# The low halves of eight input-weight blocks made by VectorE instead of TensorE, in a kernel with a written-out order

## The chip, the cores and the metric

The kernel runs on one core of one Trainium2 chip. The metric is the device time of one execution in microseconds (us), as the median of several runs. Engines are named as in the profile: PE is TensorE (PEld its weight loads), DVE is VectorE, ACT is ScalarE, POOL is GpSimd, SP is SyncE. "L603" is line 603 of the kernel. A difference of about 0.5% (3.3 us) is what a measurement of this kernel can tell from no change.

## The reference

A delta-rule linear attention runs over 768 steps for 4 batches and 8 heads of width 48. Its output, 3072 tokens of 384 values, goes through a feed-forward layer with 2048 hidden values:

```python
for t in range(S):                                   # 768 steps
    y[:, :, t] = einsum('bhd,bhde->bhe', q_t, state)
    v_old = einsum('bhde,bhd->bhe', state, k_t)      # k normalised
    state = state + b_t * outer(k_t, v_t - v_old)
x = y as (3072, 384)
h = x @ w_in                                         # 384 x 2048
g = h * erf(softplus(h))
return g @ w_out                                     # 2048 x 384
```

## The kernel before

**Two halves of the work.** The 768 steps are cut into 12 chunks of 64. For each chunk and each batch there is one step of a chain (48 steps): `chain_u`, `chain_s` and `chain_y` multiply by the state on PE (L461, L474, L488), and DVE or ACT take the results out (L467, L482, L480, L493). Ahead of each chunk a triangular system is solved row by row on POOL (`solve_row`, L363 and L364), and `merge_e` (PE, L400) puts the solved blocks together. Four chain steps give 256 tokens, a group; there are 12 groups. For a group `x_hi` (ACT, L661) and `x_lo` (DVE, L666) split the tokens into a high and a low half of 16 bits each, the tiles `xh` and `xl` (`xh0` is group 0). `ffn1` (PE, L678) computes h in 16 blocks of 128 hidden values, nine matmuls each; `e_sp` and `e_erf` (ACT, L704 and L709) apply softplus and erf, each after a load of its function table (L128) where the other stands in the engine; `e_mul`, `e_split` and `e_rest` (DVE L713; DVE L724 or ACT L722; POOL or DVE L728) form g and its two halves; `ffn2` (PE, L739 to L741) multiplies them by the output weights and sums over the 16 blocks.

**Weights.** An fp32 product is made of products of 16-bit halves, so both weight matrices are split into a high and a low half too. They come in as pairs of 32-bit words, twelve pieces each (`w_load`, DMA on SP), and are put together by `w_mask` (ACT, L539), `w_low` and `w_bits` (DVE, L543 and L547). `w_sum` (ACT, L554) and `w_max` (DVE, L558) find the largest magnitude, `w_scale` the power of two to scale by. Then each of the 16 blocks (128 x 384) is split:

- `w_hi` makes the high half `h`: mode 5 on DVE (L588), the other modes used here on ACT (L590).
- `w_lo` makes the low half, a scaled minus h. In modes 3 and 5 PE does it first: `w_dif` multiplies the block by a scaled identity `dg` in fp32 (L603) and adds the block's high half times a negative identity `ng` (L604), into a PSUM bank `wd_in` of the pool that also holds the two `ph` banks of `ffn1`; ACT then copies it to the low half (L611). In mode 0, DVE does it in one two-operand pass from SBUF (L615).

The halves of block i are written over the staged fp32 values of block i-1, so `w_hi` of a block waits until the block before has been read by `w_dif` or `w_lo`. The list `LMI` gives the mode of each of the 16 blocks of `w_in`, `LMO` of `w_out` (all 0):

```python
m = (LMI if nm == "in" else LMO)[i]
...
on(ti, w_hi, nm, i, m)
if m > 2:
    on(ti + 0.04, w_dif, nm, i)
on(ti + 0.08, w_lo, nm, i, m)
```

**Order.** Every piece of work is an event `on(time, function, arguments)`. The events are sorted by time, and then put into the order that the table `ORDER` gives; the instructions go to the engines in that order, and each engine runs its own in order. Tiles of pools wait for their readers. During the first 80 us PE is filled up with matmuls that compute nothing (`warm` and `fill`, L143), each at its place in the order.

Of the kernel before, what the change touches and what calls it, by code (L numbers as in the profile page):

```python
# [37 lines left out]
WARM = 8  # L38
WU = 150
WO = 0.6  # L40
WD = 0.4
RI = "HLHLHLHLHLLL"
RO = "HLHLHLHLHLLL"
LMI = [5, 3] * 8
LMO = [0] * 16
WG = 3
LID = 0.12
LOD = 0.25
HQ = (0, 4)
SPA = (2, 6)  # L50
# [22 lines left out]
def delta_ffn_kernel(ctx, tc, kT, qT, ktok, vtok, btok, w_in, w_out, cst, out):  # L73
# [825 lines left out]
    for nm, t in (("in", us(42)), ("out", WO + WD * (NRW - 1) + 1.2)):  # L899
# [4 lines left out]
        for i in range(NFF):  # L904
            m = (LMI if nm == "in" else LMO)[i]
            ti = t + 0.2 + (LID if nm == "in" else LOD) * i
# [42 lines left out]
    ev.sort(key=lambda e: (e[0], e[1]))  # L949
    if ORDER:  # L950
        ev = [ev[i] for i in ORDER]
    E = mybir.EngineType
# [45 lines left out]
```

## Time and profile before

| | |
|---|---|
| runs | 657.1, 657.86, 655.23 us; median 657.1 us |
| profiled execution | 655.3 us; span of the profile 653.5 us |
| PE, DVE, ACT, POOL busy | 96%, 73%, 72%, 56% of the span |
| granted PE clock, mean | 0.995 |
| first `ffn1` matmul of group 0 | 96.74 us from the start |
| first `ffn2` matmul | 128.76 us |

The span is the time between the first and last recorded instruction; the execution's own time is 1.8 us longer. Busy shares are means over stages: up to about 66 us weights are put together and the first chunks solved, from there to 97 us `w_in` is split and the first tokens are made, from 97 to 129 us the first `ffn1` blocks run while `w_out` is scaled and the third chunk solved, and after that chain and feed-forward layer run side by side to the end.

### The profile page before, as it was taken

The page shows a single profiled execution, that of the slowest core. Times are in us where ns is not written, and L with a number is a line of the kernel's source. Part 1 is how long each engine was busy: PE and PEld are TensorE (multiplying, and loading weights), DVE is VectorE, ACT ScalarE, POOL GpSimd, SP SyncE. Part 2 cuts the span into 40 slices and gives each one's busy share as a digit, 9 for nine tenths or more (in the row PEclk, how much of TensorE's full clock was granted, in tenths as well). Part 3 has the DMA queues.
Part 4 walks back from the last instruction along what each step waited for, and adds up shares of the span by engine and source line. Part 5 has one row for each costly group of instructions (what it writes and reads, how often), then busy time and mean ns, then how long its engine had stood idle before and what let it go on. Part 6 is the DMA issues. An engine that isn't in the chain of part 4 may idle for free.

```text
span 653.5 us, 22870 instructions
## 1 busy us (share of the span) xinstructions
PE 624.5 (96%) x9866; PEld 481.5 (74%) x9866; DVE 479.3 (73%) x1032; ACT 470.3 (72%) x696; POOL 364.3 (56%) x524
## 2 busy tenths in 40 slices
PE   5969999999999999999999999999999999999996
PEld 4646667788678788678787777787787787777764
DVE  4999887898889877688975868775676767565451
ACT  1468789999678765775677677688782879778851
POOL 4190388779997359694279952158986131302421
PEclk9999999999999999999999999999999999999999
DMA  9857853471113742304625034441004410000101
GB/s 233 315 188 231 194 140 87 102 151 42 41 50 98 158 73 64 75 3 106 143 52 132 2 83 94 104 84 45 16 2 87 111 33 2 1 14 2 25 17 44
DMA packets 76421, 56.19 MB, mean 86 GB/s; under 512 B 57185, under 2 KB 66529, under 8 KB 76321
## 3 DMA queue, kind: packets, MB, share of 16 engines
q1 hardware_dynamic: 76320, 54.74, 34.2%
q8 instruction: 77, 1.26, 0.8%
q14 instruction: 24, 0.19, 0.1%
HBM read 42.14 MB, written 12.58 MB: 84 GB/s over the span
## 4 chain that ended last, share of the span: by engine, by line
PE 56%; DVE 20%; ACT 13%; DMA 3%; issue 3%; POOL 2%; SPq 2%; POOLq 0%; ACTq 0%; DVEq 0%
PE ph L678 17%; PE pr L739 7%; PE pr L741 7%; PE pr L740 7%; ACT L128 4%; DVE H L713 3%; PE pc L488 2%; PE pq L251 2%; ACT L L704 2%; PE pc L461 2%; PE pg L251 2%; ACT L L709 2%; PE pc L474 2%; PE pm L426 1%; DVE z L467 1%
## 5 line engine op out<-in xcount | busy, mean ns | idle before, releaser
L678 PE MATMUL ph<-xh,w_in 128*128 128x256 f16 x1152 | 207.1, 273 | 2.6 <-ACT L L704 2.0
L678 PEld LDWEIGHTS <-w_in 128*128 128x128 f16 x1728 | 164.9, 98 | 30.0 <-issue 3.6
L728 POOL TENSOR_TENSOR L<-H,L 128x512 f16<-128x512 f32 x72 | 86.8, 1213 | 150.6 <-DVE L L724 69.0
L128 ACT ACT_TABLE_LOAD x131 | 168.1, 1283 | 2.3
L678 PE MATMUL ph<-xl,w_in 128*128 128x256 f16 x576 | 157.0, 273 | 0.0
L740 PE MATMUL pr<-w_out,L 128*128 128x384 f16 x384 | 125.2, 326 | 0.6 <-DVE w_out L615 0.6
L739 PE MATMUL pr<-w_out,L 128*128 128x384 f16 x384 | 125.4, 327 | 0.0
L741 PE MATMUL pr<-w_out,L 128*128 128x384 f16 x384 | 125.2, 326 | 0.0
L448 POOL TENSOR_TENSOR z<-v,nm 64x192 f32<-64x192 f32 x96 | 58.6, 610 | 102.1 <-DMA v<-vtok 64.9
L704 ACT ACTIVATE L<-ph,xct 128x512 f32<-128x512 f32 x96 | 65.8, 687 | 49.2 <-DVE H L691 46.1
L364 POOL TENSOR_TENSOR xb<-xb,tmp 128x31 f32<-128x31 f32 (+15 forms) x155 | 93.4, 603 | 12.1
L363 POOL TENSOR_TENSOR tmp<-gb,xb 128x31 f32<-128x31 f32 (+15 forms) x155 | 89.7, 578 | 12.1 <-DMA gb<-d 2.3
L713 DVE TENSOR_TENSOR H<-H,L 128x512 f32<-128x512 f32 x96 | 78.5, 824 | 20.9 <-ACT L L709 20.2
L691 DVE TENSOR_SCALAR H<-ph 128x512 f32<-128x512 f32 x72 | 49.1, 684 | 38.9 <-PE ph L678 35.2
L709 ACT ACTIVATE L<-L 128x512 f32<-128x512 f32 x96 | 58.3, 626 | 0.8
L741 PEld LDWEIGHTS <-L 128*128 128x128 f16 x384 | 37.6, 98 | 25.6 <-issue 0.8
L739 PEld LDWEIGHTS <-L 128*128 128x128 f16 x384 | 37.5, 98 | 21.4
L740 PEld LDWEIGHTS <-L 128*128 128x128 f16 x384 | 37.6, 98 | 20.2
L467 DVE TENSOR_TENSOR z<-pc,ga 64x192 f32<-64x192 f32 x80 | 28.4, 355 | 21.4 <-PE pc L461 19.8
L482 DVE TENSOR_TENSOR z<-pc,z 48x192 f32<-48x192 f32 x72 | 25.4, 353 | 16.7 <-PE pc L474 10.8
L724 DVE CAST L<-H 128x512 f16<-128x512 f32 x72 | 36.4, 510 | 1.6
L661 ACT ACTIVATE xh<-pt,xsx 64x128 f16<-64x128 f32 (+1 forms) x72 | 25.9, 394 | 14.3 <-DVE xsx L528 7.4
(159 smaller groups left out, 983.1 us busy)
## 6 DMA issues: line engine op xcount, KB each, us to landing
raw_in<-w_in SPq DMA_DIRECT2D x12, 512.0 KB, 7.6
raw_out<-w_out SPq DMA_DIRECT2D x12, 512.0 KB, 5.5
d<-A SPq DMA_DIRECT2D x20, 256.0 KB, 3.2
kpg<-kT SPq DMA_DIRECT2D x24, 192.0 KB, 3.9
k<-ktok SPq DMA_DIRECT2D x12, 384.0 KB, 4.1
qp<-qT SPq DMA_DIRECT2D x24, 192.0 KB, 4.0
v<-vtok SPq DMA_DIRECT2D x48, 96.0 KB, 3.3
out<-ob SPq DMA_DIRECT2D x48, 96.0 KB, 2.2
```

The source lines that it names most:

```text
L128: se.add_instruction(mybir.InstLoadActFuncSet(name=nc.get_next_instruction_name(), act_func_set_id=i, ins=[], outs=[]))
L363: ge.tensor_tensor(tv, G[:, s, s + 1:].unsqueeze(1).broadcast_to([P, ncol, nr]), Xv[:, :, s:s + 1].broadcast_to([P, ncol, nr]), op=ALU.mult)
L364: ge.tensor_tensor(Xv[:, :, s + 1:], Xv[:, :, s + 1:], tv, op=ALU.add)
L448: ge.tensor_tensor(zz[j % 6][h1, :, hb, :], vt[j][h1], st[c]["nm"][h1, cs].unsqueeze(2).broadcast_to([C, NP, D]), op=ALU.mult)
L678: te.matmul(ph, w[:, i, kt * P:kt * P + P], G[x][:, :, ksl], start=(m == 0), stop=(m == 8))
L704: se.activation(unit("L", g, u), G["ph", u], AF.Softplus, bias=0.0, scale=G["ct"])
L709: se.activation(Lu, Lu, AF.Erf, bias=0.0, scale=1.0)
L713: ve.tensor_tensor(Hu, Hu, unit("L", g, u), op=ALU.mult)
L728: (ge if (g * NFF // EU + u) % GLM else ve).tensor_tensor(G["gl", u], unit("H", g, u), G["gh", u], op=ALU.subtract)
L739: te.matmul(G["po"][a], gh[:, o, asl], wout_h[:, i, :], start=(i == 0), stop=False)
L740: te.matmul(G["po"][a], gh[:, o, asl], wout_l[:, i, :], start=False, stop=False)
L741: te.matmul(G["po"][a], gl[:, o, asl], wout_h[:, i, :], start=False, stop=(i == NFF - 1))
```

## The change

Blocks 0 to 7 of `w_in` are split as before. For blocks 8 to 15 the mode becomes 0: the high half is made by ACT (L590, where half of these blocks had it on DVE, L588), the low half by DVE's pass L615; `w_dif` and the copy L611 of these blocks are gone. All events stand in a new order.

```diff
-ORDER = (42,7,36,3,5,63,4,14,13,15,77,72,6,9,65,49,37,58,48,57,...
+ORDER = (1,442,7,42,5,3,4,27,360,14,77,6,56,273,72,15,9,65,37,49,...
...
-LMI = [5, 3] * 8
+LMI = [5, 3] * 4 + [0] * 8
```

`ORDER` had 2531 entries and has 2523: eight `w_dif` events less. By instructions: PE L603 and L604 from 16 to 8 blocks each; DVE L588 from 8 to 4 and L615 from 16 (all of `w_out`) to 24; ACT L590 for `w_in` from 8 to 12, L611 from 16 to 8, and table loads from 131 to 123, since `e_sp` and `e_erf` of neighbouring blocks stand together in more places. POOL and SP issue the same instructions as before, in another order.

On PE, just ahead of the first `ffn1` matmul: `wd_in9` to `wd_in11` are the differences of blocks 9 to 11 (two pieces, the rows between them are chain matmuls). Before:

```order
L603 MATMUL wd_in9_1616<-w_in_100,dg_103 128x384
L604 LDWEIGHTS ng_104
L604 MATMUL wd_in9_1616<-w_in_100,ng_104 128x384
L474 MATMUL pr2_83<-z5_99,k1_124 48x48 x8
L603 MATMUL wd_in10_1645<-w_in_100,dg_103 128x384
```

```order
L603 MATMUL wd_in11_1676<-w_in_100,dg_103 128x384
L604 LDWEIGHTS ng_104
L604 MATMUL wd_in11_1676<-w_in_100,ng_104 128x384
L678 LDWEIGHTS w_in_100
L678 MATMUL ph0_1_1686<-xh0_1619,w_in_100 128x256
```

After, at the same place (`pt` is the transposed tokens of group 0, from L644 and L645):

```order
L474 MATMUL pr1_82<-z4_98,k1_125 48x48 x8
L644 MATMUL pt0_1_1620<-ident_84,y2_1517 128x128
L645 MATMUL pt0_1_1620<-ident_84,y2_1517 64x128
L644 MATMUL pt0_1_1620<-ident_84,y3_1550 128x128
L645 MATMUL pt0_1_1620<-ident_84,y3_1550 64x128
L488 MATMUL pr2_83<-z5_99,qp1_0_88 64x48
```

```order
L474 MATMUL pr2_83<-z5_99,k1_125 48x48 x8
L678 LDWEIGHTS w_in_100
L678 MATMUL ph0_1_1682<-xh0_1615,w_in_100 128x256
L678 LDWEIGHTS w_in_100
L678 MATMUL ph0_1_1682<-xl0_1616,w_in_100 128x256
```

Before, twelve `w_dif` stand ahead of the first L678 and four behind it; after, all eight stand ahead of it, and between the last of them and L678 there is chain and token work alone.

On DVE, around the low half of group 0's tokens (`xl0`; `xsx0` is their scale). Before:

```order
L467 TENSOR_TENSOR z5_99<-pr2_83,ga0_254 64x4x48 x2
L588 TENSOR_SCALAR w_in_100<-w_in_100,sc_in_110 128x384
L666 SCALAR_TENSOR_TENSOR xl0_1620<-pt0_0_1499,xsx0_1561,xh0_1619 128x2x128
L666 SCALAR_TENSOR_TENSOR xl0_1620<-pt0_0_1499,xsx0_1561,xh0_1619 64x2x64 x2
L482 TENSOR_TENSOR z2_96<-pr1_82,z4_98 48x4x48 x2
L666 SCALAR_TENSOR_TENSOR xl0_1620<-pt0_1_1576,xsx0_1561,xh0_1619 128x2x128
L666 SCALAR_TENSOR_TENSOR xl0_1620<-pt0_1_1576,xsx0_1561,xh0_1619 64x2x64 x2
```

After:

```order
L467 TENSOR_TENSOR z5_99<-pr2_83,ga0_268 64x4x48 x2
L615 SCALAR_TENSOR_TENSOR w_in_100<-w_in_100,sc_in_110 128x384
L666 SCALAR_TENSOR_TENSOR xl0_1616<-pt0_0_1596,xsx0_1564,xh0_1615 128x2x128
L666 SCALAR_TENSOR_TENSOR xl0_1616<-pt0_0_1596,xsx0_1564,xh0_1615 64x2x64 x2
L615 SCALAR_TENSOR_TENSOR w_in_100<-w_in_100,sc_in_110 128x384
L666 SCALAR_TENSOR_TENSOR xl0_1616<-pt0_1_1620,xsx0_1564,xh0_1615 128x2x128
L666 SCALAR_TENSOR_TENSOR xl0_1616<-pt0_1_1620,xsx0_1564,xh0_1615 64x2x64 x2
L615 SCALAR_TENSOR_TENSOR w_in_100<-w_in_100,sc_in_110 128x384
```

Two of the new passes L615 stand between the pieces of `xl0` where one L588 and a chain pair L482 stood; L482 has moved behind.

On ACT, up to the first erf of a block that `ffn2` needs first (`L0_0` is blocks 0 and 1 of group 0). Before:

```order
L590 ACTIVATE w_in_100<-w_in_100,sc_in_110 128x384
L611 CAST w_in_100<-wd_in14_1975 128x384
L273 COPY qp1_0_88<-pq3_0_1989 64x512
L273 COPY qp1_1_89<-pq3_0_1989 64x512
L590 ACTIVATE w_out_101<-w_out_101,sc_out_114 128x384
L128 ACT_TABLE_LOAD
L709 ACTIVATE L0_0_1742<-L0_0_1742 128x512
```

After:

```order
L590 ACTIVATE w_out_101<-w_out_101,sc_out_114 128x384
L128 ACT_TABLE_LOAD
L704 ACTIVATE L0_2_2085<-ph0_4_1987,xct0_1565 128x512
L128 ACT_TABLE_LOAD
L709 ACTIVATE L0_2_2085<-L0_2_2085 128x512
L722 CAST L0_1_1818<-H0_1_1806 128x512
L709 ACTIVATE L0_0_1745<-L0_0_1745 128x512
```

Two table loads, a softplus, an erf of another block (`L0_2`) and a cast now stand directly ahead of this erf. From the last instruction of `xh0` to this erf there were 36 instructions on ACT and are 42.

2 lines of the change are left out of this document (1 added, 1 removed).

## The prediction

> **What bounds the kernel now.** I read the page's first lines first, then the table of windows cut at three milestones: 65.70 us, when DVE has the largest magnitude of `w_in`; 96.75, the first `ffn1` matmul; 128.76, the first `ffn2` matmul. Columns of the windows: stretch, its length, busy time and instructions of PE, PEld, DVE, ACT, POOL, granted clock, DMA share, GB/s.
>
> ```profile
> PE 624.5 (96%) x9866; PEld 481.5 (74%) x9866; DVE 479.3 (73%) x1032; ACT 470.3 (72%) x696; POOL 364.3 (56%) x524
> PE 56%; DVE 20%; ACT 13%; DMA 3%; issue 3%; POOL 2%; SPq 2%; POOLq 0%; ACTq 0%; DVEq 0%
> 65.70:96.75 31.05, 29.68 (x492) 20.28 (x492) 25.84 (x61) 25.06 (x57) 19.03 (x33) 1.00 0.68 166
> 96.75:128.76 32.01, 30.13 (x441) 24.98 (x440) 26.22 (x67) 31.41 (x50) 25.84 (x44) 1.00 0.42 98
> 128.76:653.50 524.74, 512.97 (x7574) 399.44 (x7571) 372.90 (x781) 380.12 (x538) 293.73 (x413) 1.00 0.28 61
> ```
>
> PE is busy 96% of the span, and idle 1.4, 1.9 and 11.8 us in the three stretches, so work taken from it should shorten the run. But in the second stretch ACT is busier than PE: 31.41 of 32.01 us. Whether PE's saving shows depends on that. The matmuls around the first milestone, by PE's timeline (start, length, what):
>
> ```profile
> 77.68 1.14 PE L143 MATMUL warm<-zero 128*128 128x384 f16 x6
> 93.75 0.91 PE L603 MATMUL wd_in<-w_in,dg 128*128 128x384 f32 x2
> 94.50 0.33 PE L604 MATMUL wd_in<-w_in,ng 128*128 128x384 f16 x1
> 94.76 0.67 PE L461 MATMUL pr<-z,xm 128*64 128x48 f32 x16
> 96.74 0.27 PE L678 MATMUL ph<-xh,w_in 128*128 128x256 f16 x1
> 78.70:96.75 18.05, 17.59 (x279) 11.87 (x278) 15.12 (x37) 15.00 (x36) 14.51 (x27) 1.00 0.60 144
> ```
>
> The last filler ends near 78.7, and from there PE is busy 17.59 of 18.05 us: it sets the first `ffn1` before. One `w_dif` costs it 94.76 - 93.75 = 1.01 us. At the second milestone the engines hand over just in time (erf on ACT, product, cast and rest on DVE, `ffn2` on PE):
>
> ```profile
> 93.78 1.10 ACT L661 ACTIVATE xh<-pt,xsx 128x256 f16<-128x256 f32 x3
> 94.90:121.75 26.85, 24.97 (x390) 20.10 (x389) 22.41 (x57) 26.35 (x40) 23.79 (x40) 1.00 0.41 94
> 119.83 1.28 ACT L128 ACT_TABLE_LOAD   x1
> 121.12 0.63 ACT L709 ACTIVATE L<-L 128x512 f32<-128x512 f32 x1
> 126.25 0.68 DVE L713 TENSOR_TENSOR H<-H,L 128x512 f32<-128x512 f32 x1
> 126.96 0.61 DVE L724 CAST L<-H 128x512 f16<-128x512 f32 x1
> 127.61 0.88 DVE L728 TENSOR_TENSOR L<-H,L 128x512 f16<-128x512 f32 x1
> 128.76 0.33 PE L739 MATMUL pr<-w_out,L 128*128 128x384 f16 x1
> ```
>
> `xh0` is done at 94.88; the first erf that `ffn2` needs ends 121.75, after 26.87 us in which ACT is busy 26.35; DVE then takes until 128.49.
>
> **The change, priced.** The prices are the means of groups (line, operation, count; busy, mean ns; idle before and its releaser):
>
> ```profile
> L603 PE MATMUL wd_in<-w_in,dg 128*128 128x384 f32 x32 | 14.2, 525 | 1.9 <-ACT L L704 1.9
> L604 PE MATMUL wd_in<-w_in,ng 128*128 128x384 f16 x16 | 5.2, 326 | 0.9 <-DVE w_in L588 0.9
> L611 ACT CAST w_in<-wd_in 128x384 f16<-128x384 f32 x16 | 7.6, 475 | 4.0 <-PE wd_in L604 3.9
> L588 DVE TENSOR_SCALAR w_in<-w_in,sc_in 128x384 f16<-128x384 f32 x8 | 4.4, 550 | 0.1
> L590 ACT ACTIVATE w_in<-w_in,sc_in 128x384 f16<-128x384 f32 x8 | 4.9, 611 | 1.3 <-PE wd_in L603 1.3
> L615 DVE SCALAR_TENSOR_TENSOR w_out<-w_out,sc_out 128x384 f16<-128x384 f32 x16 | 14.1, 884 | 4.8 <-ACT w_out L590 4.8
> L128 ACT ACT_TABLE_LOAD x131 | 168.1, 1283 | 2.3
> L482 DVE TENSOR_TENSOR z<-pr,z 48x192 f32<-48x192 f32 x8 | 2.8, 352 | 0.1
> L543 DVE TENSOR_SCALAR raw_out<-raw_out 128x512 int32<-128x512 int32 x12 | 7.4, 620 | 0.0
> ```
>
> In all: PE loses 8 x 1.01 = 8.1 us; DVE gains 8 x 0.884 - 4 x 0.55 = 4.9; ACT loses 8 x 0.475 - 4 x 0.611 = 1.4, and eight table loads, 10.3. The counts below are from the two orders.
>
> *Up to the first `ffn1`.* DVE has three instructions fewer ahead of the largest magnitude (one L543, two L467, which cost about as much as L482): 0.62 + 0.71 = 1.3 us earlier. From there to the last `xl0` it has 62 instead of 60: three L615 (2.65), one L543 (0.62) and two L467 (0.71) more, two L588 (1.10) and two L482 (0.71) fewer, +2.2. ACT has 51 in both to the last `xh0`, by kinds +1.2. PE has 8 `w_dif` there instead of 12, 4.0 us less, and fillers stand as far as the sixth `w_dif`. So PE no longer sets this point, DVE does: 25.84 + 2.2 = 28.0 us of work instead of 31.05 of stretch. If it waited for nothing, the milestone would come 31.05 - 28.0 + 1.3 = 4.3 early; if all its waits stayed, 2.2 - 1.3 = 0.9 late. PE's pieces between still release it, so a good part of the waits stays: I take 1.0 us early, range -3 to +1.
>
> A wait is new here: `w_hi` of blocks 9 to 15 (ACT) waits for L615 of the block before (DVE), and the pieces of `xh0` are queued behind three of them. The two alternate, `xh` 1.10 and L590 0.61 on ACT beside `xl` 1.09 and L615 0.88 on DVE:
>
> ```profile
> 65.55 0.16 DVE L558 TENSOR_REDUCE m_in<-mx_in 128x1 f32<-128x4 f32 x1
> 95.65 1.09 DVE L666 SCALAR_TENSOR_TENSOR xl<-pt,xsx,xh 128x256 f16<-128x256 f32 x3
> ```
>
> Per half, ACT needs 1.71 us and DVE 1.97; so ACT's wait is covered by DVE's own work: 0, at most one L590, 0.6, inside the range above.
>
> *First `ffn1` to first `ffn2`.* ACT has 42 instructions from the last `xh0` to that erf instead of 36: two table loads, a softplus, an erf, a cast and four copies among those added, five L611 among those gone; by prices +4.3. ACT had 0.5 us idle here, so the erf ends 31.2 us after `xh0` instead of 26.87. Behind it DVE needs only its three instructions, 0.68 + 0.61 + 0.88 and their starts, 2.2 to 2.9, where it took 6.7 (121.75 to 128.49). 31.2 + 2.6 = 33.8, against 128.49 - 94.88 = 33.6: no change. So of the four `w_dif` that PE loses here nothing is won. DVE has 70 instructions ahead of this L728 instead of 65, +4.0 us (five L615 4.42, two L482 0.71, less two L588 1.10), and was idle 32.01 - 26.22 = 5.8: it fits, with 1.8 left. I take 0, range -1 to +2, the upper end if DVE's own waits don't shrink.
>
> *Behind the first `ffn2`.* PE's work is the same. What waits there is short (PE's waits, engine and line waited for: us, times, mean):
>
> ```profile
> PE ph L678 <- ACT L L704: 2.0, 3, 1.0
> PE pr L740 <- DVE w_out L615: 0.6, 1, 0.6
> ```
>
> Ten of ACT's table loads fewer lie here, 12.8 us, off the path but for the first of these waits; I take -0.7 (about a third of it), range -4 to +4 since the order is new for 1,500 events and 11.8 us of PE's idle time is the stock both ways.
>
> Sum: -1.0 + 0 - 0.7 = -1.7; the profiled execution took 655.3 us (span 653.5 and 1.8 around it), so 653.6 by it. It stands 1.8 below the median of its runs, 657.1, and the measured time should be 657.1 - 1.7 = 655.4.
>
> **Rivals.** *The saving comes through.* If ACT's and DVE's work beside PE gives way, as PE's 96% suggests, all 8.1 us show: 657.1 - 8.1 = 649.0. For it speaks that PE was saturated up to 96.75; against it, ACT's 31.41 of 32.01 us right behind. It needs ACT's chain to the erf to be shorter than I add up, by about 5 us, or the loss to be taken back from the 11.8 us later.
>
> *POOL and DVE hold each other up; slower.* The same pass L615 took 0.61 us at 123.66, when POOL stood idle, and 1.59 at 129.01, beside POOL's L282:
>
> ```profile
> 123.66 0.61 DVE L615 SCALAR_TENSOR_TENSOR w_out<-w_out,sc_out 128x384 f16<-128x384 f32 x1
> 129.01 1.59 DVE L615 SCALAR_TENSOR_TENSOR w_out<-w_out,sc_out 128x384 f16<-128x384 f32 x1
> 128.93 2.81 POOL L282 TENSOR_TENSOR qp<-qp,mask 64x512 f32<-64x512 f32 x2
> L364 POOL TENSOR_TENSOR xb<-xb,tmp 128x31 f32<-128x31 f32 (+15 forms) x31 | 18.2, 587 | 2.4
> L363 POOL TENSOR_TENSOR tmp<-gb,xb 128x31 f32<-128x31 f32 (+15 forms) x31 | 16.9, 544 | 2.4
> 122.65 0.27 POOL L364 TENSOR_TENSOR xb<-xb,tmp 128x31 f32<-128x31 f32 x1
> 135.03 0.24 PE L400 MATMUL pe<-T,A 32*32 32x32 f32 x2
> ```
>
> The eight new passes fall among the 62 rows of the solve (66 to 130 us). If each holds POOL up for its own 0.61, the solve ends 8 x 0.61 = 4.9 late, at 127.8 instead of 122.9, and the merge at 135.03, which follows it through two trips of DMA, and the chain behind it follow. With the 1.0 won ahead: 657.1 + 4.9 - 1.0 = 661.0. It decides once the solve's delay exceeds what stands between its end and the merge, 12.1 us, less those trips, which this trace does not split. Against it: the mean of L615 is 0.884, so most of the passes lose 0.3 and not 1.0, and DVE's L588, taken away four times, are passes too.
>
> [...]
>
> *Stalls of the new order*, anywhere, of either sign: a part of the ranges above; as a case of its own, 3 us or more either way, 0.07.
>
> **How the numbers follow.** My forecast 0.45 (its own range 652 to 658.5, some 3 us either way: 2 from the first `ffn1` and 2 from the idle time behind `ffn2`, added as independent), the saving whole 0.28, slower by POOL and DVE 0.20, other stalls 0.07. Predicted 655.4. Low end 648: it takes in 649.0; high end 662: it takes in 661.0; outside remain the larger stalls and the far tails of each, under 2 in 10. About 0.5%, 3.3 us, is what can be told from no change: faster is below 653.8, slower above 660.4. Faster: the saving case 0.26, a fifth of my forecast 0.09, half the stalls 0.03: 0.38. Slower: most of the POOL case 0.14, 0.03 of mine, 0.03 of stalls: 0.20. Same: 0.42.
>
> **What would show it.** In the profile after: first L678 near 95.7 and no PE saturation ahead of it; PE's idle time between first `ffn1` and first `ffn2` up from 1.9 to about 6 us, waiting for ACT or DVE; the first L739 near 127.8; PE busy near 616, and its share lower; idle time behind it still near 11 to 12 us. If L739 comes at 121 to 123, the saving case holds; if the last L364 ends past 127 and L400 past 139, the POOL case. L615 for `w_in` well above 0.9 us speaks for that too. I would be wrong if ACT reached the erf sooner than by its count, or if the new order changed PE's 11.8 us of later idle time by several us.

## The result, and the profile after

The changed kernel is slower: median 665.0 us (662.12 to 669.29, 4 runs) against 656.16 for the kernel before (its three runs above and a fourth, 654.69), ratio 1.0104, 95% interval 1.0063 to 1.0145. On another chip it took 667.86, ratio 1.0129 (1.0088 to 1.0170). The forecast was 655.4, faster by 1.7, with a range of 648 to 662.

The profiled execution took 662.1 us, span 660.3. The page's first line and its chain by engine:

```profile
PE 626.5 (95%) x9842; PEld 481.9 (73%) x9842; DVE 487.6 (74%) x1036; ACT 459.7 (70%) x684; POOL 367.8 (56%) x524
PE 45%; POOL 19%; DVE 14%; ACT 11%; DMA 5%; issue 5%; SPq 1%; POOLq 0%; DVEq 0%; ACTq 0%
```

PE has 8 us less to do, yet it is busy 626.5 us where it was busy 624.5: some of its work took longer, at a lower clock (mean granted clock 0.978, before 0.995). The same three stretches as before, cut at the largest magnitude of `w_in` (64.74), the first `ffn1` (94.92) and the first `ffn2` (130.45):

```profile
64.74:94.92 30.18, 29.37 (x511) 20.51 (x506) 24.60 (x60) 25.14 (x53) 19.82 (x33) 1.00 0.73 196
94.92:130.45 35.53, 27.91 (x432) 23.29 (x429) 29.45 (x75) 34.45 (x53) 28.30 (x44) 1.00 0.35 84
130.45:660.34 529.89, 516.14 (x7572) 400.39 (x7572) 382.38 (x782) 366.45 (x526) 294.09 (x412) 0.99 0.27 60
```

The second is 3.5 us longer than before, and PE's idle time in it went from 1.9 to 7.6 us; ACT is as full as it was (34.45 of 35.53). The third is 5.1 us longer, at a mean clock of 0.99. What PE waited for in the second stretch:

```profile
101.33 0.27 PE L678 MATMUL ph<-xh,w_in 128*128 128x256 f16 x1 [1.24 <-ACT L L704]
115.76 0.27 PE L678 MATMUL ph<-xh,w_in 128*128 128x256 f16 x1 [1.41 <-ACT L L704]
123.78 0.27 PE L678 MATMUL ph<-xh,w_in 128*128 128x256 f16 x1 [1.67 <-ACT L L704]
129.04 0.39 PE L678 MATMUL ph<-xh,w_in 128*128 128x256 f16 x2 [0.81 <-DVE w_in L615]
132.12 0.34 PE L741 MATMUL pr<-w_out,L 128*128 128x384 f16 x1 [1.17 <-DVE L L728]
```

Three times `ffn1` waits for a softplus on ACT, which frees a `ph` bank; at 129.04 it waits for the new pass L615 of the last block. At the hand-over ACT's erf ends at 126.71 (first row below). DVE's five passes behind it and POOL's four mask multiplications (`gram_p2`, L282) follow:

```profile
126.09 0.62 ACT L709 ACTIVATE L<-L 128x512 f32<-128x512 f32 x1
126.75 0.69 DVE L713 TENSOR_TENSOR H<-H,L 128x512 f32<-128x512 f32 x1 [3.74 <-ACT L L709]
127.36 1.63 DVE L615 SCALAR_TENSOR_TENSOR w_in<-w_in,sc_in 128x384 f16<-128x384 f32 x1
128.91 1.48 DVE L724 CAST L<-H 128x512 f16<-128x512 f32 x1
130.43 1.64 DVE L728 TENSOR_TENSOR L<-H,L 128x512 f16<-128x512 f32 x1
131.99 1.22 DVE L638 TENSOR_TENSOR xco<-xm,c_out 128x1 f32<-128x1 f32 x1
126.96 6.22 POOL L282 TENSOR_TENSOR qp<-qp,mask 64x512 f32<-64x512 f32 x4
```

The cast took 0.61 before and takes 1.48, the rest 0.88 and now 1.64: each of the last four ends 0.0 to 0.6 us behind the end of one of the four L282. Even a pass over one column (L638) takes 1.22, where the median of its twelve is 0.15. Before, L282 began at 128.93, behind this hand-over. Then PE's clock (the column ahead of the last two):

```profile
128.00:130.00 2.00, 1.17 (x10) 0.60 (x7) 2.00 (x2) 1.95 (x7) 1.93 (x2) 1.00 0.40 62
130.00:132.00 2.00, 0.50 (x2) 0.11 (x2) 1.97 (x3) 1.12 (x1) 1.85 (x3) 1.00 0.87 178
132.00:134.00 2.00, 1.20 (x6) 0.61 (x7) 2.00 (x4) 0.00 (x0) 1.93 (x2) 0.80 0.23 51
134.00:136.00 2.00, 2.00 (x15) 0.97 (x15) 1.95 (x6) 1.19 (x2) 0.59 (x2) 0.50 0.71 111
138.00:140.00 2.00, 2.00 (x27) 1.64 (x25) 1.74 (x3) 1.95 (x4) 0.00 (x0) 0.50 0.17 39
140.00:142.00 2.00, 2.00 (x39) 1.65 (x39) 1.97 (x4) 1.56 (x3) 1.25 (x2) 0.99 0.00 0
```

After six microseconds in which PE was busy 2.9, its clock is halved until 140, about 6.8 us (below, such a stretch is called a dip): a "busy" PE that does less, an L741 taking 0.52 us in it and 0.33 behind it.

The stretches of the main profiles side by side, in us, worked out from the starts of the same instructions in each trace, the last column to the end of the last one (the time up to the largest magnitude of `w_in` is left out: it lies between 64.7 and 71.4 in the profiles of both orders, from one execution to the next):

| | to first `ffn1` | to third `ffn2` matmul | to second group's first `ffn2` | to the last `ffn2` |
|---|---|---|---|---|
| before | 31.0 | 32.4 | 52.3 | 467.0 |
| changed | 30.2 | 37.2 | 54.2 | 469.0 |
| changed, again | 30.8 | 37.4 | 54.2 | 469.4 |
| edit alone (below) | 29.9 | 34.8 | 51.3 | 467.1 |
| new order in the front alone (below) | 32.2 | 36.6 | 51.7 | 468.8 |

The two profiles of the changed kernel agree within 0.6 us in every stretch, so +4.8 between the first `ffn1` and the third `ffn2` matmul and +1.9 behind it can be read. The long rest scatters more: ten profiles with the order of before there have 466.3 to 471.7 (mean 468.6), seven with the new order 469.0 to 472.1 (mean 470.7). So some 2 us more there show as a mean, not in one profile.

### The profile page after: what moved, and what is told of

Its sections match the earlier page's. It is cut to its first block, busy times and chain, and to the rows that moved or that the text cites. A ratio compares the mean times of both kernels' runs of the same rounds, so it can differ in the third digit from the quotient of the medians.

```text
span 660.3 us, 22811 instructions
## 1 busy us (share of the span) xinstructions
PE 626.5 (95%) x9842; PEld 481.9 (73%) x9842; DVE 487.6 (74%) x1036; ACT 459.7 (70%) x684; POOL 367.8 (56%) x524
## 4 chain that ended last, share of the span: by engine, by line
PE 45%; POOL 19%; DVE 14%; ACT 11%; DMA 5%; issue 5%; SPq 1%; POOLq 0%; DVEq 0%; ACTq 0%
PE ph L678 14%; POOL xb L364 7%; POOL tmp L363 7%; PE pr L739 6%; PE pr L740 5%; PE pr L741 5%; ACT L128 4%; POOL L L728 2%; PE warm L143 2%; PE pg L251 2%; POOL z L448 2%; DMA d<-A 2%; DVE H L713 2%; ACT L L709 2%; PE pc L488 2%
## 5 line engine op out<-in xcount | busy, mean ns | idle before, releaser
L678 PE MATMUL ph<-xh,w_in 128*128 128x256 f16 x1152 | 206.4, 273 | 7.7 <-ACT L L704 5.4
L678 PEld LDWEIGHTS <-w_in 128*128 128x128 f16 x1728 | 165.6, 98 | 36.0 <-issue 6.9
L728 POOL TENSOR_TENSOR L<-H,L 128x512 f16<-128x512 f32 x72 | 87.9, 1229 | 170.7 <-DVE L L724 79.6
L678 PE MATMUL ph<-xl,w_in 128*128 128x256 f16 x576 | 157.2, 273 | 0.3 <-DVE xl L666 0.3
L741 PE MATMUL pr<-w_out,L 128*128 128x384 f16 x384 | 125.6, 327 | 1.2 <-DVE L L728 1.2
L364 POOL TENSOR_TENSOR xb<-xb,tmp 128x31 f32<-128x31 f32 (+15 forms) x155 | 95.6, 617 | 12.2
L713 DVE TENSOR_TENSOR H<-H,L 128x512 f32<-128x512 f32 x96 | 76.3, 803 | 28.5 <-ACT L L709 21.8
L691 DVE TENSOR_SCALAR H<-ph 128x512 f32<-128x512 f32 x72 | 49.1, 685 | 28.9 <-PE ph L678 21.1
L741 PEld LDWEIGHTS <-L 128*128 128x128 f16 x384 | 37.6, 98 | 27.4 <-DVE L L728 1.6
L724 DVE CAST L<-H 128x512 f16<-128x512 f32 x72 | 45.3, 633 | 1.4
L143 PE MATMUL warm<-zero 128*128 128x384 f16 x158 | 34.1, 366 | 2.2 <-issue 2.2
```

Of the source, the lines that this page charges most:

```text
L364: ge.tensor_tensor(Xv[:, :, s + 1:], Xv[:, :, s + 1:], tv, op=ALU.add)
L678: te.matmul(ph, w[:, i, kt * P:kt * P + P], G[x][:, :, ksl], start=(m == 0), stop=(m == 8))
L713: ve.tensor_tensor(Hu, Hu, unit("L", g, u), op=ALU.mult)
L728: (ge if (g * NFF // EU + u) % GLM else ve).tensor_tensor(G["gl", u], unit("H", g, u), G["gh", u], op=ALU.subtract)
L741: te.matmul(G["po"][a], gl[:, o, asl], wout_h[:, i, :], start=False, stop=(i == NFF - 1))
```

## Experiments

Beside these runs the kernel before was run 23 to 35 times on each chip, with medians of 659.0 to 660.3 us, 3 to 4 us above that of the first four. Ratios are against the runs on the same chip, and times in us are to be read through them.

**The edit, or the order?** The first kernel has the old order with the new modes; of each of blocks 8 to 15 `w_lo` stands where its `w_dif` stood:

```diff
-LMI = [5, 3] * 8
+LMI = [5, 3] * 4 + [0] * 8
 order of events, for i = 8 ... 15:
-w_dif in i
+w_lo in i
...
-w_lo in i
```

> The order of before with the new modes: blocks 8 to 15 have their low half by DVE's pass L615, standing where their w_dif stood; no other event moves. Theory, the order and not the modes made the loss: the mask multiplications stand behind the hand-over as before, the first ffn2 matmul comes at 127 to 130 us, and the time is 652 to 658 us, within 0.5% of before. Rival, the passes on DVE cost by themselves (4.9 us more on DVE, ACT's high half waiting for DVE block by block): 660 to 666 us. Rival, PE's 8 us come through with the old order: 648 to 650 us.

Measured: 659.95 us against 659.72, ratio 1.0002 (0.9976 to 1.0028). As forecast by the ratio; the hand-over is clear of POOL's masks here (L728 takes 1.00 us and ends at 134.88, the masks begin at 136.68). The edit in the old order costs nothing and brings nothing to within 0.3%, and with the same modes the new order costs 1.0 to 1.3%: the loss is the order's. Whether the new order would lose as much with the old modes was not run. Held against the edit alone, the changed kernel's profile is 2.4 us longer up to the third `ffn2` matmul, 2.9 in the next stretch and about 2 in the rest. Two more kernels split this zero. One leaves out the eight `w_dif` and puts nothing in their place, the other adds eight DVE passes and leaves PE as it was:

```diff
 def w_dif(nm, i):
     a, h, _ = w_parts(nm, i)
+    if i > 7:
+        return
...
-        se.copy(l, wt[nm]["d", i])
+        se.copy(l, h if i > 7 else wt[nm]["d", i])
```

```diff
 def w_dif(nm, i):
     a, h, l = w_parts(nm, i)
+    if i > 7:
+        ve.scalar_tensor_tensor(l, a, wt[nm]["sc"], h, op0=ALU.mult, op1=ALU.subtract)
```

> The kernel before, in its own order and modes, without the eight w_dif of blocks 8 to 15: nothing takes their place, and ACT's copy to the low half reads the high half instead of the bank (so the low halves of these blocks are not those of the reference). PE loses its 8.1 us of work, DVE and ACT do as much as before. Theory: the stretch from the first ffn1 to the first ffn2 is bound by ACT, and what PE loses there becomes idle time; the first ffn1 comes 1 to 3 us sooner, the run is 1 to 3 us shorter (ratio 0.995 to 0.999). Rival, PE was the bound and the new passes on DVE ate the gain in the run of the edit alone: 6 to 8 us shorter (ratio 0.988 to 0.991).

> The kernel before with eight DVE passes L615 added: for blocks 8 to 15 the low half is first made by DVE, then made again by w_dif and ACT's copy as before. DVE has 8 x 0.6 to 0.9 = 5 to 7 us more to do, PE and ACT the same. Theory: DVE has 5 us of idle time in each of the two stretches, and the passes cost 0 to 2 us (ratio 1.000 to 1.003). Rival, the passes hit the path of the tokens and the hand-over: 4 to 7 us longer (1.006 to 1.011).

Measured: 0.9960 (0.9933 to 0.9987), 2.6 us shorter, and 1.0039 (1.0011 to 1.0066), 2.6 us longer. So of PE's 8.1 us some 2.6 show in the end even if nothing is paid for them, and the eight passes cost 2.6: together the zero of the edit alone. The first came as the theory had it; the second lies a little above the theory's upper end and below the rival's range. The windows of the stretch from first `ffn1` to first `ffn2`, without the eight `w_dif` and with the passes added:

```profile
99.84:134.95 35.11, 30.07 (x429) 25.38 (x428) 28.85 (x75) 34.09 (x56) 26.90 (x47) 0.90 0.45 102
99.50:132.90 33.40, 30.43 (x440) 25.07 (x440) 30.19 (x74) 31.92 (x50) 26.23 (x43) 1.00 0.40 93
```

With four `w_dif` fewer in it the stretch is 3.1 us longer and not shorter (35.11, before 32.01): ACT is full in both, and in the first PE's clock averages 0.90. The first `ffn1` came 1.8 us sooner behind the magnitude (29.2, before 31.0).

**The hand-over.** In the changed kernel, the masks moved behind two additions on POOL (events by name, in the order of the table):

```diff
 put_v 8
...
-gram_p2 2 0
...
-gram_p2 2 1
...
 put_v 11
...
 put_v 9
+gram_p2 2 0
+gram_p2 2 1
```

> The changed kernel with one thing moved: the four mask multiplications of chunk 2 (POOL, L282, which ran from 126.96 to 133.18 us) stand behind the additions put_v 11 and put_v 9 on POOL instead of ahead of them. Theory: each DVE pass with two SBUF operands of the hand-over to the first ffn2 (L615 1.63 us, L728 1.64) and the cast (L724 1.48) waited for an L282 to end; without them beside it these take 0.6 to 0.9 us each, L728 ends about 2.6 us sooner, the granted clock stays at 1.0 between 133 and 140 us, and the time falls by 3 to 6 us against the changed kernel, to 659 to 662 us (ratio 1.004 to 1.009 to before). Rival, the order of ACT alone is what costs: the DVE passes get shorter but the time moves by less than 1 us. Rival, the new DVE passes themselves cost: no change.

Measured: ratio 1.0143 (1.0091 to 1.0195). DVE's passes of the hand-over, POOL's masks and a wait of PE:

```profile
134.36 0.60 DVE L615 SCALAR_TENSOR_TENSOR w_in<-w_in,sc_in 128x384 f16<-128x384 f32 x1
134.89 0.41 DVE L724 CAST L<-H 128x512 f16<-128x512 f32 x1
135.34 0.69 DVE L728 TENSOR_TENSOR L<-H,L 128x512 f16<-128x512 f32 x1
146.49 6.09 POOL L282 TENSOR_TENSOR qp<-qp,mask 64x512 f32<-64x512 f32 x4
157.39 0.27 PE L678 MATMUL ph<-xh,w_in 128*128 128x256 f16 x1 [3.15 <-ACT L L704]
```

The mechanism is as stated: without L282 beside them the three take 0.60, 0.41 and 0.69, and the stretch to the third `ffn2` matmul is 34.4 us instead of 37.2. The forecast of the time failed: the masks came 13 us later (counted from the magnitude) and ran into the next four (first row 146.49, the next four from 155.97), PE waited 3.15 us at 157, its clock was halved from 158.7 to 165.5, and the next stretch was 57.6 instead of 54.2. So the masks' price at the hand-over is shown, and that moving them shortens the run is not. With the masks behind put_v 11 alone:

> The changed kernel with the four mask multiplications of chunk 2 behind the addition put_v 11 alone on POOL, and not behind put_v 9 as well, where they came as late as 146 us and ran into the next four. Theory: the hand-over to the first ffn2 is as short as in the run with the masks late (2.8 us less than in the changed kernel), and less of it is given back later: 1 to 4 us shorter than the changed kernel (ratio to before 1.004 to 1.009). Rival, the masks meet other passes of DVE and POOL's rest wherever they stand: no shorter than the changed kernel (1.010 or more).

Measured: 1.0091 (1.0056 to 1.0126), where the changed kernel on the same chip had 1.0129: 34.5 us to the third `ffn2` matmul, 54.8 in the next stretch. The intervals of the two overlap, so the gain of 2.5 us by the ratios is likely and not shown. The erf itself moved ahead on ACT:

```diff
 w_hi out 0
...
+e_erf 0 0
...
 e_sp 0 4
...
 e_erf 0 4
...
-e_erf 0 0
...
 e_mul 0 0
+e_split 0 0
+e_rest 0 0
...
 w_lo in 15
...
-e_split 0 0
...
-e_rest 0 0
```

> The changed kernel with the erf of blocks 0 and 1 of group 0 moved on ACT ahead of the two table loads, the softplus and the erf of blocks 8 and 9 that stood ahead of it, and the cast and rest of blocks 0 and 1 on DVE moved ahead of the L615 of w_in's last block. Theory: ACT reaches this erf at about 121.8 us instead of 126.1, DVE has finished product, cast and rest by about 125.5 instead of 132.1, ahead of the mask multiplications; the first ffn2 matmuls then wait for PE's own ffn1 (about 130) and the second block of w_out (about 132). The time falls by 2 to 5 us, to 660 to 663 us. Rival, the mask multiplications delay the next DVE passes just as much: less than 1 us.

Measured: 663.34 us, 1.0057 (1.0028 to 1.0086), just below the changed kernel's second interval (from 1.0088) and overlapping its first (1.0063 to 1.0145): a gain of 3 to 5 us by the ratios, likely and not clear of the noise.

```profile
126.34 0.69 DVE L728 TENSOR_TENSOR L<-H,L 128x512 f16<-128x512 f32 x1
129.49 1.68 DVE L615 SCALAR_TENSOR_TENSOR w_in<-w_in,sc_in 128x384 f16<-128x384 f32 x1 [2.46 <-ACT w_in L590]
126.54 0.37 PE L678 MATMUL ph<-xh,w_in 128*128 128x256 f16 x1 [2.19 <-ACT L L704]
133.25 0.33 PE L739 MATMUL pr<-w_out,L 128*128 128x384 f16 x1
```

DVE's hand-over is done at 127.0, and yet `ffn2` starts at 133.25: PE's own `ffn1` blocks waited 2.19 us for the softplus on ACT that was moved back, and for the L615 of the last block, again beside L282. With one wait of this stretch gone the next stands right behind it, and ACT is in most of them. This profile is 0.8 and 2.1 us shorter in the stretches up to the second group (36.4 and 52.0) and 3.1 longer in the rest (472.1), with a dip of the clock at 287 and one at 505 that the changed kernel's profiles do not have; where the median gains is not located. The clock, in the changed kernel with PE's holes filled:

```diff
 def ffn1(n):
+    if n == 10:
+        idle(10)
...
 def ffn2(n):
+    if n == 0:
+        idle(4)
...
+    if n == 0 and a == 0:
+        idle(8)
+    if n == 1 and a == 0:
+        idle(5)
```

`idle(k)` issues k matmuls of zeros into the bank that `ffn2` of group 0 sums in.

> The changed kernel with 27 matmuls of zeros added to PE, none of which changes a result: ten ahead of the ffn1 block that waited at 123.8 us, four ahead of the first ffn2 matmul, eight between its second and third, five in the next block, 0.16 us each, in places where PE stood idle. Theory: the halved clock from 133.6 to 140 us follows from PE's idle time between 122 and 134; filled up, the clock stays at 1.0 and the time falls by the 3.2 us that the half clock cost, less what fillers push back (0 to 1.5): 662 to 664 us. Rival, the clock falls for another reason: the dip stays, and the time is the same or up to 1.5 us longer.

Measured: 664.38 us, 1.0100 (1.0054 to 1.0146), no different from the changed kernel's 1.0104 and 1.0129. From 133 to 140 us, with the holes filled and in the changed kernel:

```profile
133.00:140.00 7.00, 6.61 (x94) 4.66 (x93) 6.91 (x13) 3.97 (x6) 3.56 (x4) 1.00 0.67 125
133.00:140.00 7.00, 6.32 (x75) 4.71 (x74) 6.64 (x14) 4.44 (x7) 1.52 (x3) 0.52 0.55 89
```

The dip is gone in this profile, and it stood in both profiles of the unfilled kernel, so here PE's idle time made it; but about 1 us is won up to the second group's first `ffn2` (53.1 instead of 54.2) and 0.6 lost to the fillers ahead of it. That the half clock cost 3.2 us is wrong: DVE was busy 6.91 and 6.64 of these 7 us, and beside a full engine most of the dip cost nothing.

**Better versions, none of which came.** In the edit alone the second `ffn1` matmul waited for `xl0`, and the clock fell (to half, from 102.5 us for 3.4 us):

```profile
102.79 0.37 PE L678 MATMUL ph<-xl,w_in 128*128 128x256 f16 x1 [1.51 <-DVE xl L666]
104.00:106.00 2.00, 2.00 (x12) 1.42 (x10) 1.97 (x4) 1.98 (x4) 1.84 (x3) 0.51 0.06 20
```

Two kernels take that up by the order (events by name), the second with one more move, of a mask that costs ACT table loads:

```diff
 w_hi in 9
...
-w_lo in 9
...
-w_hi in 10
...
-w_lo in 10
...
-w_hi in 11
...
 x_lo 0 1
+w_lo in 9
...
-w_lo in 11
...
+w_hi in 10
...
+w_lo in 10
...
+w_hi in 11
...
+w_lo in 11
```

```diff
 e_sp 0 0
...
-w_mask out 9
...
 e_sp 0 2
+w_mask out 9
```

> The edit alone (order of before, new modes) with the low half of block 9 and both halves of blocks 10 and 11 moved behind the low half of group 0's tokens on DVE and ACT. In the edit alone the second ffn1 matmul waited 1.5 us for that low half, behind two L615 and a chain pair, and PE's granted clock fell to 0.5 for 4 us behind it. Theory: the wait goes, the first ffn1 block starts at full speed, and the time is 1 to 3 us below the edit alone (ratio to before 0.996 to 0.999). Rival, ACT bounds what follows and takes it back: same as the edit alone (0.999 to 1.002).

> The kernel of the run before this one (low halves late) with one more event moved: the w_mask of w_out's piece 9, which stood between two softplus and cost ACT two table loads, stands behind the second softplus, where the table it needs is loaded anyway; ACT has two table loads fewer, 2.6 us, between the first ffn1 and the first ffn2. Theory, ACT bounds that stretch: 1.5 to 2.6 us shorter than the same kernel without the move, in the stretch and in the end (ratio to before 0.992 to 0.997). Rival, another engine bounds the stretch: less than 0.7 us.

Measured: 1.0003 (0.9970 to 1.0035) and 1.0041 (1.0006 to 1.0075). The first came as its rival had it. The wait of the second matmul fell from 1.51 to 0.96 us and the dip behind it is gone, but the first `ffn1` came no more than 0.2 us sooner (29.8 us behind the magnitude, 29.9 in the edit alone), and the stretch behind it got longer, 37.2 and 40.2 us instead of 34.8. The second saved one table load and not two (133 loads instead of 134), and its clock fell at 104 and at 121 us. Both forecasts missed; that a table load less in this stretch shortens it was not shown. The hole filled with zeros:

```diff
 te.matmul(ph, w[...], G[x][...], start=(m == 0), stop=(m == 8))
 m += 1
+if n == 3 and m == 1:
+    for _ in range(14):
+        te.matmul(ph, zero[:, :P], zero[:, :GT], start=False, stop=False)
```

```diff
 def spread(col, name):
     ps = pbank(f"sp{name}")[:, :P]
+    if name == "out":
+        for _ in range(24):
+            te.matmul(ps, zero[:, :P], zero[:, :P], start=True, stop=True)
```

> The edit alone (order of before, new modes) with 14 matmuls of zeros, 0.11 us each, added into the open sum of the first ffn1 block between its first and second matmul, where PE waited 1.5 to 1.7 us for the tokens' low half; results don't change. Theory: PE's saved work became idle time, and idle time halves the granted clock for 3.4 us at a time (1.7 us lost each, at 102 us in the edit alone); with the hole filled that dip goes, ACT gets its first block 1.4 us sooner, and the run is 1 to 2 us shorter than the edit alone (ratio to before 0.997 to 0.999). Rival, ACT takes it back or the dip has another cause: no change (0.999 to 1.002).

> The kernel of the run before this one (one hole filled) with 24 short matmuls of zeros, 0.055 us each, ahead of the matmul that spreads the largest magnitude of w_out, in whose neighbourhood PE waited 1.3 and 1.7 us and its clock fell at 123 us. Theory: that dip goes too, 0.5 to 1.7 us shorter than with one hole filled (ratio to before 0.995 to 0.998). Rival, PE is not the bound there: same as with one hole filled, or up to 1 us longer, since the matmul of w_out's magnitude stands behind the fillers.

Measured: 1.0044 (1.0014 to 1.0075) and 1.0057 (1.0020 to 1.0094), slower, not faster. With one hole filled, the dip at the start of `ffn1` is gone. The second one of the edit alone (at 123.0, 22 us behind the first `ffn1`, 3.4 us long) comes at 115.6, 20 us behind it, and lasts 6.8 us:

```profile
112.00:124.00 12.00, 9.13 (x125) 7.48 (x123) 10.48 (x31) 11.81 (x20) 10.51 (x20) 0.72 0.38 71
```

ACT is busy 11.81 of these 12 us and PE 9.13: what the first fillers saved PE was not the limit here, and PE stood idle further on. With both holes filled a dip of 3.4 us is still left at 118.9. No kernel here with the new modes beats the one before.

**Which part of the order?** Three kernels with the new modes splice the two orders:

```
first:  events up to the second ffn2 block in the new order, the rest in the old one
second: events up to the second ffn2 block in the old order, the rest in the new one
third:  events up to w_max of w_in in the new order, the rest in the old one
```

The changed kernel was run again, too (the fourth text).

> The new modes, with all events up to the second ffn2 block in the new order and all that follow in the order of before. Theory, most of the loss lies between the first ffn1 and the first ffn2 (ACT's longer queue, DVE beside the mask multiplications) and in the clock behind it: 4 to 7 us slower than before (ratio 1.006 to 1.010). Rival, the loss lies in the later order: within 0.3% of before.

> The new modes, with all events up to the second ffn2 block in the order of before and all that follow in the new order. Theory: 1 to 3 us slower than before (ratio 1.001 to 1.005). Rival, the loss lies in the later order: 6 us or more slower (1.009 or more).

> The new modes, with the events up to the largest magnitude of w_in (the first 66 us) in the new order and all that follow in the order of before. Theory: PE is not the bound there, its low clock costs nothing, and the time is that of the edit alone, 0.997 to 1.003 to before. Rival, the low clock of the new front (some 10 us of full clock lost ahead of 66 us in the profiles, against 2 to 7 in the old one) delays the largest magnitude: 3 to 6 us slower (1.005 to 1.009).

> The changed kernel itself, on the same chip as these runs, so that the parts can be held against it. All theories: 1.006 to 1.015 to before, and the stretches from the largest magnitude of w_in on as in its first profile within 0.2 us, but for stretches in which the granted clock falls in one of the two and not in the other, which differ by 1.7 us or a multiple.

Measured: new order early 1.0091 (1.0054 to 1.0127); late 1.0044 (1.0010 to 1.0077); in the front alone 1.0049 (1.0020 to 1.0077); the changed kernel again 1.0129. Early and late add up to it within the intervals, 0.9% and 0.4%. The forecasts for early and late held; the one for the front did not: against the edit alone (1.0002, on another chip) it costs some 3 us, and of the early part only about as much again is left for what the order does from the magnitude to the first `ffn2`. In the early kernel the masks begin at 132.49, so that of the three passes only L728 runs beside them: L615, L724 and L728 take 0.86, 0.72 and 1.63 us, and the third `ffn2` matmul comes after 35.8 us instead of 37.2. The changed kernel's stretches agreed with its first profile within 0.6 us, not within 0.2 as forecast. The clock in the front, in the changed kernel and before:

```profile
13.00:24.00 11.00, 9.75 (x145) 7.52 (x145) 10.10 (x31) 2.50 (x4) 0.00 (x0) 0.53 1.03 352
13.00:24.00 11.00, 10.23 (x151) 6.93 (x151) 10.18 (x32) 2.62 (x5) 0.00 (x0) 1.00 1.04 312
```

In the new front PE ran at half clock nearly throughout this stretch, and again from 34 to 45 us. The 1.00 of the second row says less than it seems to: the clock's records begin at 19.3 us in the trace of before (at 10.3 in the changed kernel's), and time ahead of them counts as full. The fillers of before show it:

```profile
14.88 2.74 PE L143 MATMUL warm<-zero 128*128 128x384 f16 x8 [0.38 <-DVE zero L134]
22.92 3.26 PE L143 MATMUL warm<-zero 128*128 128x384 f16 x19
```

The first eight start 0.32 us apart, the nineteen 0.16 us apart: there too PE was slow up to about 19 us, and at full clock from there to 46.6.

The half clock does not seem to be what the front costs. The magnitude of `w_in` came at 64.7 to 71.4 us in eight profiles with the new front (mean 68.1) and at 65.5 to 71.1 in nine with the old one (mean 67.6). The front-alone profile and that of the edit alone have it at 71.38 and 71.11, and nearly all that the first is longer stands behind it (the table of stretches above). Their two stretches from there to the first `ffn1`:

```profile
71.38:103.55 32.17, 29.27 (x518) 20.60 (x515) 23.43 (x59) 22.14 (x49) 16.79 (x29) 1.00 0.63 159
71.11:101.00 29.89, 26.73 (x501) 19.14 (x498) 23.70 (x57) 23.28 (x52) 17.98 (x29) 1.00 0.64 160
```

PE, not DVE or ACT, has more to do in the first. Of the 150 fillers, the new order puts 108 ahead of the magnitude and 42 behind it, the old one 123 and 27. Fifteen more at 0.16 us are some 2.4 us of PE work in this stretch, which is 2.3 us longer. That fits most of the 3 us; no run took the fillers away, so it is not shown.

## Why the prediction was wrong

- *First `ffn1` 1.0 earlier.* It came 1.8 earlier in the profile (94.92 instead of 96.74), about half of it ahead of the magnitude. That half is luck: the time to the magnitude scatters by 6 us in the profiles of either order. The sum behind it did not hold. DVE was to have 28.0 us of work in the stretch; to the last `xl0` it is busy about 25.7. The first matmul needs only `xh0`, and starts 0.02 us behind it (94.90). And of the 4.0 us that four `w_dif` fewer take from PE here, fifteen more fillers give some 2.4 back: PE is still busy 29.37 of 30.18 us. The prediction noted how far the fillers reach, and not how many stand here; nor did it ask what their places do to PE's clock.
- *First `ffn1` to first `ffn2`: 0, range -1 to +2.* Measured +3.5, and +4.8 to the third matmul. ACT's part was about right: the erf was to end 31.2 us behind `xh0` and ended 126.71 - 94.90 = 31.8 behind it. The step that failed is the next: "Behind it DVE needs only its three instructions, 0.68 + 0.61 + 0.88 and their starts, 2.2 to 2.9". They took 5.4 (126.71 to 132.07), with the last L615 of `w_in` among them and all but the first beside POOL's masks. Without the masks beside them L615, L724 and L728 took 0.60, 0.41 and 0.69. The rows for it stood in the prediction (L615 1.59 beside L282); it sought the victims among the solve rows and took no account of where L282 itself stands in the new order. The sum has a second flaw: this stretch is counted from `xh0`, which ended at 94.90 as it had at 94.88, so the 1.0 won at the first `ffn1` could not be carried on into it.
- *POOL and DVE hold each other up*, the rival on the slow side at 0.20, had the mechanism and the wrong place. That the measured time lies beyond its 661.0 is no success of its sum: the solve ended sooner (121.86, before 122.92), and seven of the eight new passes took 0.60 to 0.88 us. That POOL loses the 0.61 us of each pass, the 4.9 of that sum, no run shows: beside seven of the passes one solve row each took 0.20 to 0.43 us more than the median of its shape, 1.9 together. What the trace shows the other way: three passes with two SBUF inputs (L615, L728, L638) end in turn 0.0 to 0.6 us behind an L282, at 1.63, 1.64 and 1.22 us, and the cast, with one input, did the same, at 1.48. In the trace of before two L691, whose operand lies in PSUM, ran beside L282 (130.27 to 131.73) at their usual 0.68 each:

```profile
130.53 1.28 DVE L691 TENSOR_SCALAR H<-ph 128x512 f32<-128x512 f32 x2
```

- *Behind the first `ffn2`: -0.7, range -4 to +4.* Measured +3.8 (524.8 instead of 519.6 from the first `ffn2` to the last, less the 1.3 that the third matmul waited): 1.9 with a clock dip at 133 us and 2.0 in the long rest, which one profile can't tell from scatter; the kernel with the new order late, 0.4% slower, says that something is lost there. The term was a guess at a third of a wait, and the ten table loads fewer shortened nothing that shows.
- *The saving comes through whole* was refuted: PE's eight `w_dif` taken away free of charge bring 2.6 us of 8.1, and the passes on DVE cost 2.6, where I had counted on idle time of 5 us in each stretch to hide them.
- The range ended at 662, on one mishap's price of 4.9 less 1.0. The new order moved 2,500 events, and the case of its stalls, either sign, had 0.07.

**Still open:** whether the fillers are what the front costs, and which waits make up the loss in the long rest.

## What to carry to other kernels

Work taken from the fullest engine need not show in the time where another is full beside it (here 2.6 of 8.1 us did): cut the profile at the hand-overs and add up each engine there before counting on a share of 96%. A reordering is a change by itself: run the edit in the old order and split the order at a hand-over, before explaining anything by the edit. Count the fillers of both orders in each stretch, for they are work too. When a DVE pass on the path reads its operands from SBUF, look up what POOL does at that moment in the new order, instruction by instruction: here L615, L724 and L728 took 0.60, 0.41 and 0.69 us clear of L282, and 1.63, 1.48 and 1.64 beside it.

## What the runs showed of the hardware

PE's granted clock in these profiles is 1.0 or 0.5: the dips last about 3.4 us or a multiple (3.4 or 6.8 behind 70 us, 10.2 in the front of the changed kernel), 1.7 us of full clock lost for each 3.4. Behind 70 us and ahead of the end of the work, in 17 profiles, a dip was the more frequent, the less PE was busy in the emptiest 3.4 us of a hole: below 1.6 us one followed in 18 of 23 holes, between 1.6 and 2.2 in 10 of 42, above 2.2 in none of 40 (a dip behind two holes counts with both). All changes of the clock in a profile lie a multiple of 3.41 us apart. Cut on that grid, the 3.41 us straight ahead of each of the 27 dips held 0.49 to 2.22 us of PE work, and no piece with more was followed by one; with 1.4 or less there was always one. The kernel before never went below 2.40 there and ran at full clock from 50.0 to 650.8 us, where its work runs out. The kernel with eight passes more had one such hole in a place where none of its work had changed:

```profile
232.00:236.00 4.00, 2.37 (x47) 1.90 (x47) 3.10 (x8) 2.06 (x6) 0.00 (x0) 1.00 1.09 162
236.00:240.00 4.00, 4.00 (x57) 3.04 (x55) 1.28 (x3) 2.60 (x3) 3.02 (x4) 0.57 0.76 162
```

The 3.4 us ahead of a dip need not be idle: a PE busy 2.2 of them was still slowed now and then (at 505.6 us with the new order late).
